# Half-partition loads, one collecting product a unit, and two result stores in a windowed decode attention kernel

## The chip, the cores and the metric

The kernel runs on one core of a Trainium2 chip. The metric is device time in microseconds (us) of one execution. The kernel before takes 218.12 us (median of three runs, 217.67 to 219.65).

A core has five engines that run their own instruction streams and wait for each other through semaphores: PE (TensorE, matrix products; PEld is its loading of weights), DVE (VectorE), ACT (ScalarE), POOL (GpSimd) and SP (SyncE, which here only issues loads and stores). Sixteen DMA engines carry the loads and stores. SBUF, the working memory, has 128 partitions; PSUM takes the products.

## The reference, cut to what matters

Everything is float32. One token for each of two batches (B = 2) goes through a layer norm, then through an attention with 32 query heads on 8 key-value heads over the last 4096 positions of a cache, and through a gated MLP whose result is the gate.

```python
W = min(4096, max(256, Sk // 4))                     # 4096 of 32768 positions
q = (x @ wq).reshape(B, Sq, Hq, Dh).transpose(0, 2, 1, 3)
k = jnp.repeat(k_cache[:, :, Sk - W:, :], rep, axis=1)
v = jnp.repeat(v_cache[:, :, Sk - W:, :], rep, axis=1)
p = _softmax(jnp.einsum("bhqd,bhkd->bhqk", q, k) * (Dh ** -0.5), axis=-1)
o = jnp.einsum("bhqk,bhkd->bhqd", p, v)
s = o.transpose(0, 2, 1, 3).reshape(B, Sq, Hq * Dh) @ wo

z = _gelu(xn @ w_in); z2 = _layernorm(z[..., Fh:])
g = _silu((z[..., :Fh] * (w_sp * z2 + b_sp)) @ w_out)
return x + s * g
```

The inputs that count by size: `w_in` 512 x 1792, `w_out` 896 x 512, `wq` 512 x 4096, `wo` 4096 x 512, and the used 4096 positions of both caches, 8 heads x 2 batches x 4096 x 128 each.

## The kernel before, in words

**Units and loads.** A unit is one key-value head with both batches. Its keys and its values are one load each of 128 partitions x 32 KB (4 MB). SP issues all large loads in one fixed order (lines 94 to 140 and 477 to 485): `win` (3.5 MB), `wout` (1.75 MB), `wq` in two loads of 4 MB, then keys and values of the eight units, the values behind the keys, and at the end `wo`: one load of 4 MB for the first set of units and six smaller ones (1 MB three times, 512 KB, 256 KB twice) for the other two sets. `win`, the two `wq`, all keys and values and the two `wo` tiles share a ring of four slots of 32 KB a partition (`slot`, line 83): a load whose slot is not yet free makes SP wait, and with it every load behind it. Loads also share eight completion semaphores in turn, so a load can wait until the one eight before it has landed.

**Head.** PE computes `z` from `win`, the four slices of the query product from `wq` (`queries`, line 238), and the gate from `wout`.

**One unit.** DVE turns the keys in four pieces (`turn`, 128 x 2048 each), PE makes the scores (16 products), DVE takes the masked row maximum (`row_max`), PE and DVE share it over the groups of rows that hold the same head (`share_max`, `bias`), ACT takes the exponential with the row sums `p.l` (`probs`, line 367), PE reorders the probabilities (`swapped`, which also sums `p.l` over the groups into column NB of `p.mo`), DVE transposes them and makes the weights `p.w = diag / sum` (`probs_t`, lines 382 to 385). Then PE multiplies by the values (`values`, 16 products into `acc`), ACT copies `acc` to `o` with the scale `p.w` (`evacuate`, line 399), and PE collects `o` (`collect`, line 409).

**Collecting.** Units form three sets: units 0 to 3, 4 and 5, 6 and 7 (`SETS`, line 329). For each unit `collect` makes four products, one for each group of 32 rows, into the tile `col`, which adds up over a set; at a set's end DVE reduces `col` to `both` and multiplies by a batch mask to `o1`. `spread` then places the columns for the product with `wo` into `oT`.

**Order.** Every instruction stands in program order on its engine (`InOrder`, line 27). The loop at line 460 interleaves: while unit n is loaded and scored, unit n-1 gets its probabilities and, behind it, its values.

**End.** After the last unit's values (line 505), `evacuate` runs on ACT and DVE in turn, then come the last `collect` and `spread`, then the products with `wo`: `wo_early` for the first 24 tiles of 128 x 512 into `part`, a copy, and four products by `rowm` into `so`; the last eight tiles go straight into `so`. Two DVE instructions (`res`) and one store of eight rows, which lie 16 partitions apart, end the kernel.

## Time and profile before

| what | value |
|---|---|
| median of the runs | 218.12 us |
| the profiled execution's own time | 218.11 us |
| its span, first to last instruction | 216.2 us |
| PE busy | 136.8 us (63%) |
| DVE busy | 103.9 us (48%) |
| ACT busy | 23.9 us (11%) |
| mean busy share of the DMA engines | 97%, 89.4 MB read |
| mean granted TensorE clock | 0.783 |

The page gives busy times of each engine, then the span in 40 equal slices as tenths, then the DMA queues, then the chain of work that ended last. Another view groups the instructions by form, with the mean time of one and what ended the idle time before them; another gives busy time, DMA share and GB/s for chosen stretches. The execution's own time is 1.9 us over its span.

### The profile page before, as it was taken

The numbers are of one execution on the slowest core, as the hardware profiler recorded it, in microseconds if no ns is written. First come the engines' busy times: TensorE is split into PE (matmuls) and PEld (weight loads), VectorE is DVE, ScalarE is ACT, GpSimd is POOL, SyncE is SP. The second block draws the span as 40 slices with busy tenths as digits, with TensorE's granted clock in tenths as the row PEclk, the third lists the DMA queues.
The fourth block names the chain that finished last, engine by engine and source line by source line (L and its number), as shares of the span: only waits on it lengthen the run. The fifth ranks groups of instructions, "written<-read, shape, count | busy, mean of one in ns | idle before, by whom it ended". The sixth has DMA issues, their size and how long they took to land.

```text
span 216.2 us, 2192 instructions
## 1 busy us (share of the span) xinstructions
PE 136.8 (63%) x908; PEld 46.8 (22%) x908; DVE 103.9 (48%) x161; ACT 23.9 (11%) x60; POOL 3.2 (1%) x16
## 2 busy tenths in 40 slices
PE   0172294627765964984593298359667749969683
PEld 0120021113112222222131122122221122342331
DVE  2504014439539638728908921990487197220201
ACT  5003003200001011021021002101010012030010
POOL 5000000000000000000000000000000000000000
PEclk9998569985587595596599559956955787997998
DMA  7999999999999999999999999999999999999990
GB/s 255 425 437 467 406 455 418 423 443 412 455 400 461 409 455 412 436 430 424 449 403 455 412 449 415 430 436 418 455 408 449 418 443 415 443 430 402 409 376 27
DMA packets 3929, 89.54 MB, mean 414 GB/s; under 512 B 446, under 2 KB 462, under 8 KB 848
## 3 DMA queue, kind: packets, MB, share of 16 engines
q1 hardware_dynamic: 3900, 89.40, 96.8%
q8 instruction: 7, 0.11, 0.2%
q10 hardware_dynamic: 20, 0.01, 0.0%
q14 instruction: 2, 0.02, 0.0%
HBM read 89.40 MB, written 0.00 MB: 413 GB/s over the span
## 4 chain that ended last, share of the span: by engine, by line
DMA 62%; DVE 17%; PE 17%; SPq 2%; issue 1%; ACT 0%; DVEq 0%; ACTq 0%
DMA v<-in_A_v_cache_dram 29%; DMA k<-in_A_k_cache_dram 20%; DVE kt L37 13%; DMA wo<-in_A_wo_dram 12%; PE acc L37 9%; PE s L37 7%; SPq L37 2%; PE pp L37 1%; DVE sm L37 1%; DVE pT L37 1%; DVE qw L37 1%; ACT p L37 0%; DVE mg L37 0%; DVE res L37 0%; PE so L37 0%
## 5 line engine op out<-in xcount | busy, mean ns | idle before, releaser
L37 DVE STREAM_TRANSPOSE kt<-k 128x2048 f32<-128x2048 f32 x32 | 72.7, 2293 | 3.4 <-DMA k<-in_A_k_cache_dram 3.4
L37 PE MATMUL acc<-v,pT 128*32 128x512 f32 x256 | 45.3, 863 | 10.9 <-DMA v<-in_A_v_cache_dram 9.6
L37 PE MATMUL s<-kt,qw 128*32 128x512 f32 x256 | 41.1, 684 | 3.7 <-DVE kt L37 3.1
L37 PE MATMUL pp<-p,swap 128*128 128x512 f32 x16 | 12.6, 880 | 21.0 <-ACT p L37 21.0
L37 DVE CUSTOM_DVE_ANT_1 sm<-s,own 128x512 f32<-128x512 f32 x8 | 5.5, 690 | 36.9 <-PE s L37 36.9
L37 PEld LDWEIGHTS acc<-v,pT 128*32 128x32 f32 x256 | 11.5, 159 | 37.4 <-issue 33.4
L37 ACT ACTIVATE o<-acc,wd 128x128 f32<-128x128 f32 x30 | 8.7, 368 | 73.9 <-PE acc L37 67.1
L37 PE MATMUL q_ps<-wq,xnT 128*32 128x512 f32 x64 | 9.6, 723 | 11.2 <-DMA wq<-in_A_wq_dram 11.2
L37 PEld LDWEIGHTS s<-kt,qw 128*32 128x32 f32 x256 | 9.4, 122 | 33.0 <-issue 21.9
L37 ACT ACTIVATE p<-sm,nb 128x512 f32<-128x512 f32 x8 | 5.8, 723 | 69.1 <-DVE nb L37 69.1
L37 DVE STREAM_TRANSPOSE pT<-pp 128x512 f32<-128x512 f32 x8 | 5.7, 706 | 5.8 <-PE pp L37 5.8
L37 PE MATMUL z<-win,xnT 128*32 128x448 f32 x32 | 5.6, 868 | 4.4 <-DMA win<-in_B_w_in_dram 4.4
L37 PE MATMUL mo<-mg,same 128*128 128x16 f32 x16 | 3.2, 273 | 7.7 <-DVE mg L37 7.7
L37 PEld LDWEIGHTS pp<-p,swap 128*128 128x128 f32 x16 | 3.0, 234 | 21.8 <-ACT p L37 21.8
L37 DVE TENSOR_REDUCE both<-col 128x32 f32<-128x128 f32 x3 | 0.9, 292 | 13.4 <-PE col L37 13.4
L37 PEld LDWEIGHTS mo<-l,same 128*128 128x128 f32 x16 | 4.4, 276 | 6.0 <-issue 6.0
L37 ACT ACT_TABLE_LOAD x4 | 5.1, 1283 | 2.6 <-POOL place L206 2.6
L37 PE MATMUL part<-wo,oT 128*32 128x512 f32 x48 | 5.4, 594 | 0.0
L37 PEld LDWEIGHTS q_ps<-wq,xnT 128*32 128x32 f32 x64 | 1.9, 125 | 14.7 <-DMA wq<-in_A_wq_dram 11.4
L37 PE MATMUL xnT_ps<-ident,xn 2*128 2x2 f32 x4 | 0.6, 253 | 7.0 <-DVE xn L37 7.0
L37 PE MATMUL qj_ps<-qT,selj 128*128 128x64 f32 x8 | 2.0, 428 | 4.8 <-DVE qT L37 4.8
L37 DVE STREAM_TRANSPOSE zt<-z 128x448 f32<-128x448 f32 x1 | 1.0, 975 | 8.3 <-ACT z L37 8.3
(106 smaller groups left out, 66.9 us busy)
## 6 DMA issues: line engine op xcount, KB each, us to landing
k<-in_A_k_cache_dram SPq DMA_DIRECT2D x8, 4096.0 KB, 26.4
v<-in_A_v_cache_dram SPq DMA_DIRECT2D x8, 4096.0 KB, 29.7
wq<-in_A_wq_dram SPq DMA_DIRECT2D x2, 4096.0 KB, 24.2
wo<-in_A_wo_dram SPq DMA_DIRECT2D x1, 4096.0 KB
win<-in_B_w_in_dram SPq DMA_DIRECT2D x1, 3584.0 KB, 11.1
wo<-in_A_wo_dram SPq DMA_DIRECT2D x3, 1024.0 KB, 21.7
wout<-in_B_w_out_dram SPq DMA_DIRECT2D x1, 1792.0 KB, 14.9
wo<-in_A_wo_dram SPq DMA_DIRECT2D x1, 512.0 KB
```

The source lines that it names most:

```text
L37: return self.tc.keep_in_program_order(call(*args, **kwargs))
```

## The change

Five things are edited.

1. `wout`, both `wq` loads and the first `wo` tile are loaded by `halves`: one load into partitions 0 to 63 and one into partitions 64 to 127, one behind the other on SP. `win`, the keys, the values and the second `wo` tile are loaded as before.
2. The first `wo` tile is also cut in two pieces of eight 128 x 512 tiles, so it comes in four loads of 1 MB. Its first piece's products (`wo_early(0)`) stand ahead of the last `collect`.
3. For units 0 to 5 `collect` makes one product of 128 x 512 with 128 weight columns in place of four of 128 columns with 32 weight columns; at the end of sets 0 and 1 DVE takes the diagonal blocks out by four reductions of 32 partitions. Units 6 and 7 collect as before.
4. The row sums are no longer divided out unit by unit. `probs` puts them in a column of the set's tile `lt`; at the set's end one product sums them over the groups, and DVE multiplies by `diag`, reduces, takes the reciprocal and applies it with the batch mask in one instruction. `evacuate` scales by the constant `diag`, so the product by `p.l`, the reciprocal `w` and the tile `wd` of each unit go.
5. The result's eight rows stand on two runs of four partitions (30 to 33 and 94 to 97) in place of eight partitions 16 apart; `x4` is loaded and the result is stored in two pieces, the stores by ACT and SP. The tiles `hT`, `oT` and `rowp` have padding columns for this.

```diff
+    def halves(dst, src):
+        for r in (slice(0, P // 2), slice(P // 2, P)):
+            sp.dma_start(dst[r], src[r])
...
-    sp.dma_start(wout, w_out.rearrange("(p j) d -> p j d", p=P))
+    halves(wout, w_out.rearrange("(p j) d -> p j d", p=P))
...
-        sp.dma_start(t, wq_v[:, a : a + 2, :])
+        halves(t, wq_v[:, a : a + 2, :])
...
+    for _, g in PAIRS:
+        act.dma_start(pair(x4, g), of_pair(x, g))
...
     def swapped(p):
         p.pp = bank(f"pp{p.n}", 512)
         pe.matmul(p.pp, swap.rearrange("p g e c -> p (g e c)"), p.p, start=True, stop=True)
-        pe.matmul(p.mo[:, NB : NB + 1], same.rearrange("p n e -> p (n e)"), p.l, start=True, stop=True)
 
     def probs_t(p):
         p.pT = sb.tile([P, CT, 32], F32, tag="pT", name=f"pT{p.n}", bufs=3)
         dve.transpose(p.pT.rearrange("p t m -> p (t m)"), p.pp)
-        w = sb.tile([P, 1], F32, tag="w", name=f"w{p.n}")
-        dve.reciprocal(w, p.mo[:, NB : NB + 1])
-        p.w = sb.tile([P, CH], F32, tag="wd", name=f"wd{p.n}", bufs=3)
-        dve.tensor_scalar_mul(p.w, diag, w)
...
-                act.activation(p.o[:, a, :], p.acc[:, a, :], AF.Copy, scale=p.w[:, a : a + 1])
+                act.activation(p.o[:, a, :], p.acc[:, a, :], AF.Copy, scale=diag[:, a : a + 1])
...
+        if whole:
             pe.matmul(
-                col[0][32 * g : 32 * g + 32], selw[:, SL - E * a0 : SL - E * a0 + 32], p.o[:, :, 32 * g : 32 * g + 32],
-                start=(a0 == 0), stop=(a0 == n - 1),
+                c.rearrange("p a d -> p (a d)"), selw[:, SL - E * a0 : SL - E * a0 + P],
+                p.o.rearrange("p a d -> p (a d)"), start=(a0 == 0), stop=(a0 == n - 1),
             )
...
         if a0 == n - 1:
+            pl = ps.tile([P, 512], F32, tag="mo", name=f"pl{p.n}")[:, :CH]
+            pe.matmul(pl, same.rearrange("p n e -> p (n e)"), lt, start=True, stop=True)
+            lsum = sb.tile([P, CH], F32, tag="lsum", name=f"lsum{p.n}")
+            dve.tensor_mul(lsum, pl, diag)
+            rl = sb.tile([P, 1], F32, tag="rl", name=f"rl{p.n}")
+            dve.reduce_sum(rl, lsum, axis=AX.X)
+            dve.reciprocal(rl, rl)
...
-            for j, n in (((0, 16),), ((0, 4), (4, 4)), ((0, 4), (4, 2), (6, 1), (7, 1)))[i]:
-                sp.dma_start(t[:, a : a + n, :], wo_s[i][:, j : j + n, :])
+            for j, n in (((0, 8), (8, 8)), ((0, 4), (4, 4)), ((0, 4), (4, 2), (6, 1), (7, 1)))[i]:
+                (sp.dma_start if i else halves)(t[:, a : a + n, :], wo_s[i][:, j : j + n, :])
...
     evacuate(units[-1], split=True)
+    wo_early(0)
     gathered(units[-1])
     spread_after(units[-1])
-    for n in range(3):
+    for n in range(1, 4):
         wo_early(n)
...
-    sp.dma_start(bass.AP(tensor=out.tensor, offset=out.offset, ap=by_group), res[0 : P : P // (G * B), :])
+    for engine, g in PAIRS:
+        engine.dma_start(of_pair(out, g), pair(res, g))
```

The loads as SP issues them, from the last values on, before (the shape is partitions x elements; `v_113` is the last unit's values, `wo_836` the first set's tile, `wo_838` the tile of the other two sets):

```order
L37 DMA v_113<-in_A_v_cache_dram 128x1x8192
L37 DMA wo_836<-in_A_wo_dram 128x8192
L37 DMA wo_838<-in_A_wo_dram 128x2048 x3
L37 DMA wo_838<-in_A_wo_dram 128x1024
L37 DMA wo_838<-in_A_wo_dram 128x512 x2
L37 DMA out_dram<-res 4x2x128
```

The first `wo` tile is one load of 128 partitions there. In the changed kernel the same stretch of SP's program reads (`v_117` is the last unit's values, `wo_801` the first set's tile, `wo_806` the other):

```order
L37 DMA v_117<-in_A_v_cache_dram 128x1x8192
L37 DMA wo_801<-in_A_wo_dram 64x4096 x4
L37 DMA wo_806<-in_A_wo_dram 128x2048 x3
L37 DMA wo_806<-in_A_wo_dram 128x1024
L37 DMA wo_806<-in_A_wo_dram 128x512 x2
L37 DMA out_dram<-res 2x2x128
```

The one load has become four of 64 partitions, and half of the result's store has left SP for ACT. The head of SP's program changes in the same way; in the changed kernel, from its first load to the first values (`v_91`), it is:

```order
L37 DMA win<-in_B_w_in_dram 128x7168
L37 DMA wout<-in_B_w_out_dram 64x3584 x2
L37 DMA wq_74<-in_A_wq_dram 64x8192 x2
L37 DMA wq_77<-in_A_wq_dram 64x8192 x2
L37 DMA k_87<-in_A_k_cache_dram 128x1x8192
L37 DMA k_89<-in_A_k_cache_dram 128x1x8192
L37 DMA v_91<-in_A_v_cache_dram 128x1x8192
```

Before, the second to fourth of these rows are single loads of 128 partitions; the order of the tiles is the same. On PE the end of the program before is, from the last unit's values (`acc_907`) to the last product (`col` collects, `oT_ps` spreads, `part` and `so` are the products with `wo`):

```order
L37 MATMUL acc_907<-v_113,pT_890 32x512 x16
L37 MATMUL col_902<-o_924,selw 32x128 x4
L37 MATMUL oT_ps_936<-o_2_329,place_258 128x16 x4
L37 MATMUL part<-wo_836,oT_324 32x512 x16
L37 MATMUL part<-wo_838,oT_327 32x512 x8
L37 MATMUL so<-parts,rowm 32x128 x4
L37 MATMUL so<-wo_838,oT_330 32x128 x32
```

And in the changed kernel, from the last unit's values (`acc_876`):

```order
L37 MATMUL acc_876<-v_117,pT_863 32x512 x16
L37 MATMUL part<-wo_801,oT_332 32x512 x8
L37 MATMUL col_871<-o_893,selw 32x4x32 x4
L37 MATMUL pl_910<-lt_340,same 128x4
L37 MATMUL oT_ps_920<-o_2_339,place_264 128x16 x4
L37 MATMUL part<-wo_801,oT_332 32x512 x8
L37 MATMUL part<-wo_806,oT_337 32x512 x8
L37 MATMUL so<-parts,rowp 32x128 x4
L37 MATMUL so<-wo_806,oT_342 32x128 x32
```

Eight of the sixteen products with the first `wo` tile now stand between the last values and the last collecting products, and the product `pl` stands behind these.

More of the change, by code (lines that the diff above doesn't have):

```diff
@@ L106, with turn_of @@
     act.dma_start(wb1[:, 1:2], bass.AP(tensor=b_sp.tensor, offset=b_sp.offset, ap=[[1, 1], [1, 1]]))
+    PAD = 32 - B
+    PAIRS = ((act, 0), (sp, 2))
+    pair = lambda t, g: t[32 * g + PAD : 32 * g + PAD + 2 * B, :]
+    of_pair = lambda t, g: bass.AP(tensor=t.tensor, offset=t.offset + g * DC, ap=[[DC, 2], [D, B], [1, DC]])
     x4 = cst.tile([P, DC], F32, tag="x4", name="x4")
     nc.gpsimd.memset(x4, 0.0)
-    by_group = [[DC, G], [D, B], [1, DC]]
-    act.dma_start(x4[0 : P : P // (G * B), :], bass.AP(tensor=x.tensor, offset=x.offset, ap=by_group))
+    for _, g in PAIRS:
+        act.dma_start(pair(x4, g), of_pair(x, g))
+    def turn_of(t, j, g):
+        return t[:, 32 * j + PAD * (g % 2) : 32 * j + PAD * (g % 2) + 32]
     def load(name, src, u):
@@ L144 @@
     make_identity(nc, ident)
-    SL = (CH - 1) * E
-    selw = cst.tile([P, SL + 32 + SL - 0], F32, tag="selw", name="selw")
+    SL = 32
+    selw = cst.tile([P, SL + P], F32, tag="selw", name="selw")
     nc.gpsimd.memset(selw, 0.0)
@@ L151 @@
     nc.gpsimd.memset(ones, 1.0)
-    hT = cst.tile([P, FT, 32], F32, tag="hT", name="hT")
+    hT = cst.tile([P, PAD + 32 * FT], F32, tag="hT", name="hT")
     nc.gpsimd.memset(hT, 0.0)
-    rowm = cst.tile([P, 32], F32, tag="rowm", name="rowm")
+    rowp = cst.tile([P, PAD + 32], F32, tag="rowp", name="rowp")
+    nc.gpsimd.memset(rowp, 0.0)
+    rowm = rowp[:, PAD:]
     dve.tensor_reduce(rowm, ident.rearrange("p (g c) -> p c g", g=G), axis=AX.X, op=ALU.add)
@@ L187 @@
     dve.tensor_copy(same, free_ap(selw, SL, [[0, NB], [1, E]]))
+    dve.tensor_copy(free_ap(selw, 2 * SL, [[32, G - 1], [1, E]]), free_ap(selw, SL, [[0, G - 1], [1, E]]))
     blk = cst.tile([P, G], F32, tag="blk", name="blk")
@@ L279 @@
     dve.tensor_scalar(z2, z2, wb[:, 0:1], wb[:, 1:2], op0=ALU.mult, op1=ALU.add)
-    dve.tensor_mul(hT[:, :, 0 : 16 * B : 16], z1, z2)
+    dve.tensor_mul(hT[:, PAD:].rearrange("p (j c) -> p j c", c=32)[:, :, :B], z1, z2)
     queries(2)
@@ L286 @@
         g = j % G
-        pe.matmul(py[32 * g : 32 * g + 32, :], hT[:, j, :], wout[:, j, :], start=(j < G), stop=(j + G >= FT))
+        pe.matmul(py[32 * g : 32 * g + 32, :], turn_of(hT, j, 1), wout[:, j, :], start=(j < G), stop=(j + G >= FT))
     ys = sb.tile([P, D], F32, tag="o", name="ys", bufs=1)
@@ L291 @@
     for g in range(G):
-        pe.matmul(y[32 * g : 32 * g + 32, :], rowm, ys[:, g * DC : (g + 1) * DC], start=True, stop=True)
+        pe.matmul(y[32 * g : 32 * g + 32, :], turn_of(rowp, 0, g), ys[:, g * DC : (g + 1) * DC], start=True, stop=True)
     gate = cst.tile([P, DC], F32, tag="gate", name="gate")
@@ L332 @@
         o1 = cst.tile([P, B, 32], F32, tag=f"o1_{i}", name=f"o1_{i}")
-        oT = cst.tile([P, nj, 32], F32, tag=f"oT_{i}", name=f"oT_{i}")
+        lt = cst.tile([P, CH], F32, tag=f"lt_{i}", name=f"lt_{i}")
+        nc.gpsimd.memset(lt, 1.0)
+        oT = cst.tile([P, PAD + 32 * nj], F32, tag=f"oT_{i}", name=f"oT_{i}")
         nc.gpsimd.memset(oT, 0.0)
         for a in range(n):
-            sets[kv + a] = (a, n, o1)
+            sets[kv + a] = (a, n, o1, lt)
         sets[f"oT{i}"] = (o1, oT, nj)
@@ L368, in probs @@
         p.p = sb.tile([P, CT * 32], F32, tag="p", name=f"p{p.n}", bufs=1)
-        p.l = sb.tile([P, 1], F32, tag="l", name=f"l{p.n}")
+        a0, _, _, lt = sets[p.n]
         act.activation(
-            p.p, p.sm.rearrange("p t y -> p (t y)"), AF.Exp, bias=p.nb, scale=SCALE, accum_out=p.l,
+            p.p, p.sm.rearrange("p t y -> p (t y)"), AF.Exp, bias=p.nb, scale=SCALE, accum_out=lt[:, a0 : a0 + 1],
         )
@@ L402, in evacuate @@
             if split and a % 2:
-                dve.tensor_scalar_mul(p.o[:, a, :], p.acc[:, a, :], p.w[:, a : a + 1])
+                dve.tensor_scalar_mul(p.o[:, a, :], p.acc[:, a, :], diag[:, a : a + 1])
             else:
-                act.activation(p.o[:, a, :], p.acc[:, a, :], AF.Copy, scale=p.w[:, a : a + 1])
+                act.activation(p.o[:, a, :], p.acc[:, a, :], AF.Copy, scale=diag[:, a : a + 1])
     col = {}
     def collect(p):
-        a0, n, o1 = sets[p.n]
+        a0, n, o1, lt = sets[p.n]
@@ L411, in collect @@
+        whole = p.n < SETS[-1][0]
         if a0 == 0:
-            col[0] = ps.tile([P, CH, 32], F32, tag="col", name=f"col{p.n}")
-        for g in range(G):
+            col[0] = ps.tile([P, CH, DH], F32, tag="col", name=f"col{p.n}")
+        c = col[0]
+        if whole:
             pe.matmul(
-                col[0][32 * g : 32 * g + 32], selw[:, SL - E * a0 : SL - E * a0 + 32], p.o[:, :, 32 * g : 32 * g + 32],
-                start=(a0 == 0), stop=(a0 == n - 1),
-            )
-        if a0 == n - 1:
-            both = sb.tile([P, 32], F32, tag="both", name=f"both{p.n}", bufs=1)
-            dve.reduce_sum(both, col[0].rearrange("p a j -> p j a"), axis=AX.X)
-            dve.tensor_mul(o1, free_ap(both, 0, [[0, B], [1, 32]]), free_ap(ofb, 0, [[1, B], [0, 32]]))
+                c.rearrange("p a d -> p (a d)"), selw[:, SL - E * a0 : SL - E * a0 + P],
+                p.o.rearrange("p a d -> p (a d)"), start=(a0 == 0), stop=(a0 == n - 1),
+            )
+        else:
+            for g in range(G):
+                pe.matmul(
+                    c[32 * g : 32 * g + 32, :, :32], selw[:, SL - E * a0 : SL - E * a0 + 32],
+                    p.o[:, :, 32 * g : 32 * g + 32], start=(a0 == 0), stop=(a0 == n - 1),
+                )
@@ new lines, in collect @@
+        if a0 == n - 1:
+            pl = ps.tile([P, 512], F32, tag="mo", name=f"pl{p.n}")[:, :CH]
[5 more added lines that the diff above has]
+            dve.reciprocal(rl, rl)
+            both = sb.tile([P, 32], F32, tag="both", name=f"both{p.n}", bufs=1)
+            if whole:
+                for g in range(G):
+                    rows, cols = slice(32 * g, 32 * g + 32), slice(32 * g, 32 * g + 32)
+                    dve.reduce_sum(both[rows], c[rows, :, cols].rearrange("p a j -> p j a"), axis=AX.X)
+            else:
+                dve.reduce_sum(both, c[:, :, :32].rearrange("p a j -> p j a"), axis=AX.X)
+            dve.scalar_tensor_tensor(
+                out=o1, in0=free_ap(both, 0, [[0, B], [1, 32]]), scalar=rl, in1=free_ap(ofb, 0, [[1, B], [0, 32]]),
+                op0=ALU.mult, op1=ALU.mult,
+            )
@@ L432, in spread @@
             )
-        dve.tensor_copy(oT[:, :, 0 : 16 * B : 16], pt.rearrange("p b j -> p j b"))
+        dve.tensor_copy(oT[:, PAD:].rearrange("p (j c) -> p j c", c=32)[:, :, :B], pt.rearrange("p b j -> p j b"))
     ends = {kv + n - 1: i for i, (kv, n, nj) in enumerate(SETS)}
@@ L494, in wo_early @@
             pe.matmul(
-                part[32 * g : 32 * g + 32, :], oT[:, j + a, :], t[:, a, :], start=(done < G), stop=(done >= EARLY - G)
+                part[32 * g : 32 * g + 32, :], turn_of(oT, j + a, 1), t[:, a, :], start=(done < G), stop=(done >= EARLY - G)
             )
@@ L514 @@
     for g in range(G):
-        pe.matmul(so[32 * g : 32 * g + 32, :], rowm, parts[:, g * DC : (g + 1) * DC], start=True, stop=False)
-    for n in range(3, len(blocks)):
+        pe.matmul(so[32 * g : 32 * g + 32, :], turn_of(rowp, 0, g), parts[:, g * DC : (g + 1) * DC], start=True, stop=False)
+    for n in range(4, len(blocks)):
         t, oT, j = blocks[n]
@@ L520 @@
                 pe.matmul(
-                    so[32 * g : 32 * g + 32, :], oT[:, j + a, :], t[:, a, g * DC : (g + 1) * DC],
-                    start=False, stop=(j + a == oT.shape[1] - 1),
+                    so[32 * g : 32 * g + 32, :], turn_of(oT, j + a, g), t[:, a, g * DC : (g + 1) * DC],
+                    start=False, stop=(n == len(blocks) - 1 and a == t.shape[1] - 1),
                 )
```

## The prediction

> **What bounds the kernel now.** I read the page first: its slices of DMA and GB/s, then the chain that ended last, then the DMA issues; after that the stretches of the span, and last the instructions at the end. The page:

> ```profile
> span 216.2 us, 2192 instructions
> PE 136.8 (63%) x908; PEld 46.8 (22%) x908; DVE 103.9 (48%) x161; ACT 23.9 (11%) x60; POOL 3.2 (1%) x16
> DMA  7999999999999999999999999999999999999990
> GB/s 255 425 437 467 406 455 418 423 443 412 455 400 461 409 455 412 436 430 424 449 403 455 412 449 415 430 436 418 455 408 449 418 443 415 443 430 402 409 376 27
> DMA 62%; DVE 17%; PE 17%; SPq 2%; issue 1%; ACT 0%; DVEq 0%; ACTq 0%
> ```

> No compute engine is near full. The DMA engines are over 90% busy in 38 of 40 slices, and only the first and the last slice are below. So the time is a ramp, a stream without a gap, and what follows the last landing. The stretches (microseconds from the span's start, then busy time of PE, PEld, DVE, ACT and POOL, granted clock, DMA share, GB/s) give the stream's rate:

> ```profile
> 16.10:25.80 9.70, 1.72 (x14) 0.52 (x6) 2.62 (x10) 2.05 (x3) 0.00 (x0) 0.71 1.00 432
> 11.80:35.50 23.70, 12.39 (x70) 3.69 (x70) 4.42 (x21) 3.74 (x6) 0.00 (x0) 0.78 1.01 436
> 35.50:192.70 157.20, 107.09 (x648) 35.55 (x649) 91.78 (x110) 15.89 (x47) 0.00 (x0) 0.75 1.00 430
> 192.70:202.40 9.70, 7.34 (x59) 2.90 (x58) 2.41 (x8) 0.73 (x2) 0.00 (x0) 0.82 0.97 413
> 202.40:212.50 10.10, 8.93 (x120) 3.95 (x120) 0.18 (x1) 0.60 (x1) 0.00 (x0) 1.00 0.84 340
> 212.50:216.20 3.70, 0.42 (x8) 0.16 (x8) 0.58 (x2) 0.00 (x0) 0.00 (x0) 0.80 0.00 1
> ```

> From 11.8 to 192.7 us the share is 1.00 and the rate 430 to 436 GB/s, whatever is loaded: 27 GB/s for each of 16 engines that are all busy. Any microsecond that the engines lose in the stream is a microsecond of the kernel.

> How far the compute side may fall behind without being seen is in the DMA issues (KB each, median us from issue to landing):

> ```profile
> k<-in_A_k_cache_dram SPq DMA_DIRECT2D x8, 4096.0 KB, 26.4
> v<-in_A_v_cache_dram SPq DMA_DIRECT2D x8, 4096.0 KB, 29.7
> wq<-in_A_wq_dram SPq DMA_DIRECT2D x2, 4096.0 KB, 24.2
> win<-in_B_w_in_dram SPq DMA_DIRECT2D x1, 3584.0 KB, 11.1
> wout<-in_B_w_out_dram SPq DMA_DIRECT2D x1, 1792.0 KB, 14.9
> ```

> 4 MB take 9.7 us at 432 GB/s, but land 26.4 us after their issue: 16.7 us of other loads lie ahead. A slot that comes free some microseconds later starves nothing. The end, in order of time (start, us, engine):

> ```profile
> 185.47 26.99 DMA wo<-in_A_wo_dram
> 212.46 0.04 issue
> 212.50 0.47 PE so L37 x8
> ...
> 213.00 0.30 DVE res L37
> 213.30 0.02 issue
> 213.32 0.29 DVE res L37
> ```

> The last piece of `wo` lands at 212.46; eight matrix instructions, two of DVE and the store follow, 3.7 us to the span's end at 216.2. The profiled execution took 218.11 us by its own time, 1.9 us over its span, and 218.12 is the median of the runs, so sums made on it carry over without a shift.

> **The change, part by part.** *The halves.* Stretch 11.8 to 35.5 is exactly `wout` and both `wq` (`win` lands at 0.7 + 11.1 = 11.8): 10.2 MB in 23.7 us. Stretch 192.7 to 202.4 is the first `wo` tile: 4.2 MB in 9.7 us. All 33.4 us become loads of 64 partitions, one half behind the other. The trace has no wide load into fewer than 128 partitions, so I bound the cost. Lower end: an engine carries 27 GB/s whatever its partitions, a half of 2 MB takes 4.85 us, and nothing is lost: 0 us. Upper end: the ceiling belongs to the ways into the partitions. In every row above each of 16 engines has an eighth of a 128-partition tile to itself; when all 16 are sent to 64 partitions, two share a way, each gets 13.5 GB/s, and 33.4 us become 66.8: +33.4 us. The reading that chooses is the rate: it is 432 for the 32 KB rows of `wq`, which lie side by side in memory, and 430 over keys and values, which alternate between two batches far apart. A limit that doesn't move with the source's layout sits rather at the engine or at the destination, and these two the trace cannot part. I take the upper end, because a half changes just what those rows have in common, all partitions at once.

> [...]

> From the upper end I take off what engines out of step give back. If of two that share a way one is t us ahead, it runs alone for t at the start of a half, and has gone over to the other half while its partner still finishes: each half costs t less. In the stretch of 202.4 to 212.5 the share is 0.84: an engine is idle for 0.16 x 10.1 = 1.6 us on average, which is how far engines lie apart there; in the stretches up to 192.7 shares of 1.00 leave a few tenths. Six halves early at 0.2 us give 1.2, four late ones at some 0.3 us (partners less apart than the whole field, and the slowest pair sets the end) give 1.2. Halves: 33.4 - 2.4 = **+31 us**. There is no cover: nothing else is bound.

> *The extra issues.* SP issues five more loads, and the second half of the first `wq` now waits for `win` to land, since eight loads share eight semaphores; `wo`'s last pieces wait so for its first halves. Rows for an issue:

> ```profile
> 1.18 0.41 SPq L37 DMA_DIRECT2D wout<-in_B_w_out_dram  x1
> 1.63 1.25 SPq L37 DMA_DIRECT2D wq<-in_A_wq_dram  x2
> ```

> 0.4 to 0.6 us each, with the whole of `wout` and half a `wq` still queued at 11.8 us, and 3 MB of `wo` when its first halves land. 0 us; without that cover, one issue, 0.6 us.

> *Collecting and sums.* The rows (mean ns of one):

> ```profile
> L37 PE MATMUL col<-o,selw 128*32 128x128 f32 x64 | 3.8, 285 | 1.7 <-DVE o L37 1.7
> L37 PE MATMUL pp<-p,swap 128*128 128x512 f32 x16 | 12.6, 880 | 21.0 <-ACT p L37 21.0
> L37 PE MATMUL mo<-l,same 128*128 128x1 f32 x16 | 3.0, 258 | 0.0
> L37 DVE RECIPROCAL w<-mo 128x1 f32<-128x1 f32 x8 | 1.0, 130 | 0.0
> L37 DVE TENSOR_SCALAR wd<-diag,w 128x4 f32<-128x4 f32 x8 | 1.8, 230 | 0.3
> L37 DVE TENSOR_REDUCE both<-col 128x32 f32<-128x128 f32 x3 | 0.9, 292 | 13.4 <-PE col L37 13.4
> ```

> A product of 128 x 512 with 128 columns is the form of `pp`: 12.6 / 8 = 1.6 us, for 3.8 / 8 = 0.5 before: six times +1.1 = 6.6 us of PE. Eight products by `p.l` go, -3.0, and three `pl` come, at most +1.1: PE +4.7 us of 136.8. DVE loses 8 x 0.36 = 2.9 us, and gains per set a multiply, a reduce and a reciprocal (0.5 us by rows of that size) and, in two sets, three more reductions of 0.29: 1.5 + 1.7 = 3.2. All this lies in a stream with 16.7 us queued ahead: 0 us. Only the last set could be seen: `pl` and 0.5 us of DVE ahead of the last `spread`, while eight early products (half of 16 x 0.11 x 2) fill PE's idle before the last `collect`. The products then still wait for `wo`: in the row above, the last ones start 0.04 us behind the landing. 0 us; without that wait, some +0.8 - 1.8 = -1 us.

> *Store and rows.* Two stores of 2 KB on two engines replace one of 4 KB, whose row is

> ```profile
> 213.64 0.69 SPq L37 DMA_DIRECT2D out_dram<-res  x1
> ```

> Between -0.3 (half the rows to issue) and +0.7 (one behind the other); I take 0, as they are issued side by side. One more `x4` load costs ACT some 0.6 us ahead of the layer norm, which has the 4.4 us that PE waits for `win`:

> ```profile
> L37 PE MATMUL z<-win,xnT 128*32 128x448 f32 x32 | 5.6, 868 | 4.4 <-DMA win<-in_B_w_in_dram 4.4
> ```

> Sum: 218.1 + 31 = **249 us**.

> **The rivals.** *The engine is the limit, not the way (not slower).* Then halves run at 432 GB/s, and everything else is under the stream: 218.1, with the store's bounds 217.8 to 219. For it: an engine at 27 GB/s is at the same figure in every row, which a limit of its own would give too. Against it: nothing in the trace, only the choice above. It decides as soon as two engines at one way get over 13.5 GB/s each; at 27 all cost is gone. Within it the end may gain: engines lie apart by 1.6 us in the last stretch, and if halves hand the late ones' rows round, up to 1.6 us go: 216.5, still under 1%.

> *The engines fall out of step.* If one of each pair is favoured, or they start 1.6 us apart from the beginning, a half of `wout` (2.1 us) costs 0.5, of `wq` (4.85) 3.25, a quarter of `wo` (2.4) 0.8: 1 + 13 + 3.2 = 17 us, 235 us. Against it: the shares of 1.00 and more in the early stretches.

> *A new wait shows.* The load order is the same, but a semaphore of eight comes round sooner; if SP were late with the first keys, the stream would have a gap of one landing, about 2 to 5 us: 221 to 223. Against it: at each such wait more than 2 MB are queued.

> **How the numbers follow.** Shared ways at nearly half rate: 0.61, 245 to 252. Out of step or in part: 0.06, 225 to 245. Engine-limited, unchanged: 0.29, 217 to 219.5. A new wait: 0.02. Faster by over 1%: 0.02; the stream's bytes and rate leave no room for 2.2 us but by the end alone. The range must hold the second case too: 217 to 252; the likeliest alone has 245 to 252. 1% is about what a measurement of this kernel tells from no change: faster 0.02, same 0.29, slower 0.69.

> **What would show it.** In the changed profile the stretches of `wout`, `wq` and the first `wo` tile have 200 to 230 GB/s with a DMA share still near 1 (engines wait with a packet in hand), the first keys land near 69 us in place of 46.6, keys and values run at 430 again, and the end behind the last landing is 3.7 us. If those stretches show 430, the rival holds and the step that took the upper end is wrong. I am also wrong if keys and values run slower than before, if DMA shares fall below 0.9 between loads (a wait), or if the last products of `so` no longer follow a landing.

## The result, and the profile after

The changed kernel takes 255.4 us (median of six runs, 254.41 to 256.33) against 218.2 us: a ratio of 1.169 (95% interval 1.164 to 1.174), +37 us. The forecast was 249 us with a range up to 252: the direction came, and the main mechanism with it, but the price was set too low. The profiled execution took 256.24 us by its own time, over a span of 254.4.

The page of the changed kernel, with the lines that were shown of before:

```profile
span 254.4 us, 2120 instructions
PE 140.8 (55%) x862; PEld 45.0 (18%) x862; DVE 104.7 (41%) x161; ACT 23.9 (9%) x60; POOL 3.5 (1%) x20
DMA  7999999898999999999999999999999999999990
GB/s 289 368 228 229 206 206 227 185 232 316 443 404 422 443 453 410 417 443 443 428 417 430 453 422 422 433 443 425 428 429 443 425 422 397 198 214 207 274 371 29
DMA 66%; PE 17%; DVE 13%; ACT 1%; issue 1%; SPq 1%; another core or an unknown queue 0%; ACTq 0%; DVEq 0%
...
wq<-in_A_wq_dram SPq DMA_DIRECT2D x4, 2048.0 KB, 28.1
wo<-in_A_wo_dram SPq DMA_DIRECT2D x7, 1024.0 KB, 37.3
```

The DMA line reads as before: 8 or 9 tenths from the second slice to the last but one. The line under it does not. In slices 3 to 9 and 35 to 37 the same busy engines move 185 to 232 GB/s. The trace's records of single packets show how both can be: over `wq` each of the 256 packets of 32 KB took 1.21 us before, and 2.57 us in the median now, and all of that time counts as busy. GB/s shows what the share hides. It isn't that fewer engines carry a half: the share, 1.00 over `wq`, is a mean over all sixteen. The trace also has sixteen completion marks (semaphore updates that report a load's end) for each of these loads, as it has for a whole one; over `wout` and `wq` the first and the last of them lie 1.0 us apart.

The stretches of the same execution, cut at the landings of `win` (12.8), `wout` (21.0), `wq` (60.9), the first keys (70.5), the values of unit 6 (208.0) and of unit 7 (220.5), the first `wo` tile (240.6) and the rest of `wo` (250.4); columns as before:

```profile
12.80:21.00 8.20, 5.11 (x34) 1.70 (x34) 2.13 (x9) 1.02 (x3) 0.00 (x0) 1.00 1.02 221
21.00:60.90 39.90, 7.22 (x36) 2.04 (x36) 3.67 (x21) 2.73 (x4) 0.00 (x0) 0.57 1.00 213
60.90:70.50 9.60, 7.49 (x56) 2.30 (x57) 2.38 (x6) 1.50 (x3) 0.00 (x0) 0.84 0.99 427
70.50:208.00 137.50, 92.53 (x504) 27.00 (x506) 85.75 (x82) 12.54 (x38) 0.00 (x0) 0.76 1.00 432
208.00:220.50 12.50, 8.43 (x65) 3.64 (x56) 3.81 (x14) 1.84 (x6) 0.00 (x0) 0.88 1.01 329
220.50:240.60 20.10, 10.77 (x66) 4.77 (x66) 1.83 (x8) 0.73 (x2) 0.00 (x0) 0.67 0.99 222
240.60:250.40 9.80, 8.28 (x97) 2.84 (x97) 0.00 (x0) 0.60 (x1) 0.00 (x0) 0.78 0.76 306
250.40:254.40 4.00, 0.42 (x8) 0.15 (x8) 0.58 (x2) 0.00 (x0) 0.00 (x0) 1.00 0.00 1
```

Two stretches of before that the prediction doesn't show by themselves, `wout` and the last values:

```profile
11.80:16.10 4.30, 4.14 (x24) 1.35 (x28) 0.00 (x0) 0.00 (x0) 0.00 (x0) 1.00 1.05 452
183.00:192.70 9.70, 8.05 (x73) 3.07 (x66) 1.54 (x6) 2.57 (x9) 0.00 (x0) 1.00 1.01 432
```

Set against before, the span's 38.2 us come out piece by piece. `win` lands 1.0 later. `wout` takes 8.2 in place of 4.3 (+3.9). Both `wq` take 39.9 in place of 19.4 (+20.5). From there to the landing of the last values the stream takes 159.6 in place of 157.2 (+2.4), and all of that is the last piece: 12.5 us for a load of 4 MB that takes 9.7 everywhere else. The first `wo` tile takes 20.1 in place of 9.7 (+10.4); the rest of `wo` 9.8 in place of 10.1 (-0.3); what follows the last landing 4.0 in place of 3.7 (+0.3). The sum is 38.2.

The last values' load is not cut in halves. It is the one ahead of halves, and the shared rate of 329 GB/s shows that it ran into them. Its completion marks say the same: the first comes 9.8 us behind the first of the load before it (205.8 to 215.6), so the leading engine lost nothing, and the last 12.5 us behind the last (208.0 to 220.5). PE waited 2.5 us for it:

```profile
220.65 5.50 PE L37 MATMUL acc<-v,pT 128*32 128x512 f32 x32 [2.53 <-DMA v<-in_A_v_cache_dram]
```

### The profile page after: what moved, and what is told of

The parts are those of the page before. It is cut to its first block, busy times and chain, and to the rows that moved or that the text cites. A ratio compares the mean times of both kernels' runs of the same rounds, so it can differ in the third digit from the quotient of the medians.

```text
span 254.4 us, 2120 instructions
## 1 busy us (share of the span) xinstructions
PE 140.8 (55%) x862; PEld 45.0 (18%) x862; DVE 104.7 (41%) x161; ACT 23.9 (9%) x60; POOL 3.5 (1%) x20
## 4 chain that ended last, share of the span: by engine, by line
DMA 66%; PE 17%; DVE 13%; ACT 1%; issue 1%; SPq 1%; another core or an unknown queue 0%; ACTq 0%; DVEq 0%
DMA v<-in_A_v_cache_dram 25%; DMA wq<-in_A_wq_dram 18%; DMA wo<-in_A_wo_dram 18%; DVE kt L37 9%; PE acc L37 7%; PE s L37 5%; DMA win<-in_B_w_in_dram 5%; PE pp L37 2%; PE q_ps L37 1%; ACT p L37 1%; DVE pT L37 1%; DVE sm L37 1%; DVE gate L37 1%; PE ys L37 1%; SPq L37 1%
## 5 line engine op out<-in xcount | busy, mean ns | idle before, releaser
L37 DVE STREAM_TRANSPOSE kt<-k 128x2048 f32<-128x2048 f32 x32 | 72.5, 2286 | 0.3 <-DMA k<-in_A_k_cache_dram 0.3
L37 PE MATMUL acc<-v,pT 128*32 128x512 f32 x256 | 43.8, 845 | 16.1 <-DMA v<-in_A_v_cache_dram 12.3
L37 PE MATMUL s<-kt,qw 128*32 128x512 f32 x256 | 38.9, 654 | 4.4 <-DVE kt L37 2.9
L37 PE MATMUL q_ps<-wq,xnT 128*32 128x512 f32 x64 | 11.7, 871 | 35.7 <-DMA wq<-in_A_wq_dram 35.7
L37 PE MATMUL pp<-p,swap 128*128 128x512 f32 x16 | 11.4, 798 | 21.2 <-ACT p L37 21.2
L37 DVE CUSTOM_DVE_ANT_1 sm<-s,own 128x512 f32<-128x512 f32 x8 | 5.5, 692 | 37.5 <-PE s L37 37.4
L37 PEld LDWEIGHTS acc<-v,pT 128*32 128x32 f32 x256 | 11.2, 158 | 47.2 <-issue 40.7
L37 ACT ACTIVATE o<-acc,diag 128x128 f32<-128x128 f32 x30 | 8.7, 367 | 77.0 <-PE acc L37 76.6
L37 PEld LDWEIGHTS s<-kt,qw 128*32 128x32 f32 x256 | 9.3, 118 | 32.1 <-issue 20.7
L37 PE MATMUL part<-wo,oT 128*32 128x512 f32 x48 | 8.1, 827 | 8.2 <-DMA wo<-in_A_wo_dram 8.2
L37 ACT ACTIVATE p<-sm,nb 128x512 f32<-128x512 f32 x8 | 5.8, 723 | 65.6 <-DVE nb L37 65.6
L37 DVE TENSOR_REDUCE mean<-mean_ps 128x2 f32<-128x14 f32 x1 | 0.2, 173 | 23.7 <-PE mean_ps L37 23.7
L37 PEld LDWEIGHTS q_ps<-wq,xnT 128*32 128x32 f32 x64 | 2.5, 145 | 40.2 <-issue 40.2
L37 DVE TENSOR_TENSOR lsum<-pl,diag 128x4 f32<-128x4 f32 x3 | 0.5, 162 | 19.6 <-PE pl L37 19.6
L37 PE MATMUL col<-o,selw 128*32 128x128 f32 (+1 forms) x28 | 8.1, 510 | 0.0
L37 DVE STREAM_TRANSPOSE pT<-pp 128x512 f32<-128x512 f32 x8 | 5.7, 714 | 4.6 <-PE pp L37 4.4
L37 PE MATMUL z<-win,xnT 128*32 128x448 f32 x32 | 4.8, 763 | 4.6 <-DMA win<-in_B_w_in_dram 4.6
L37 PEld LDWEIGHTS pp<-p,swap 128*128 128x128 f32 x16 | 2.8, 219 | 22.0 <-ACT p L37 22.0
L37 PE MATMUL mo<-mg,same 128*128 128x16 f32 x16 | 3.2, 273 | 5.8 <-DVE mg L37 5.4
L37 DVE TENSOR_SCALAR gate<-y 128x128 f32<-128x128 f32 x1 | 0.3, 291 | 14.6 <-PE y L37 14.6
L37 DVE TENSOR_TENSOR res<-so,gate 128x128 f32<-128x128 f32 x1 | 0.3, 291 | 14.2 <-PE so L37 14.2
## 6 DMA issues: line engine op xcount, KB each, us to landing
k<-in_A_k_cache_dram SPq DMA_DIRECT2D x8, 4096.0 KB, 23.5
v<-in_A_v_cache_dram SPq DMA_DIRECT2D x8, 4096.0 KB, 25.2
win<-in_B_w_in_dram SPq DMA_DIRECT2D x1, 3584.0 KB, 12.1
```

The source lines that it names most:

```text
L37: return self.tc.keep_in_program_order(call(*args, **kwargs))
```

## The experiments

**Is it the halves? Taken back, and alone.** The first run keeps the whole change but loads whole tiles:

```diff
     def halves(dst, src):
-        for r in (slice(0, P // 2), slice(P // 2, P)):
-            sp.dma_start(dst[r], src[r])
+        sp.dma_start(dst, src)
```

> The changed kernel with the halves taken back: wout, both wq and the two pieces of the first wo tile are single loads of 128 partitions; everything else of the change stays. Theory A (a load into 64 partitions runs at half rate, and this is the whole loss): 218 us, 217.5 to 219, wq at 430 GB/s, first keys landing at 46.6 us. Theory B (collecting, sums, early products or the two stores cost part of the 37 us): 221 us or more, with the excess behind 192 us of the trace.

Measured: 218.65 us, ratio 1.0016 (1.0004 to 1.0029). Its stretches of `wout`, of `wq` and about the first `wo` tile:

```profile
12.20:16.50 4.30, 4.16 (x24) 1.35 (x28) 0.00 (x0) 0.00 (x0) 0.00 (x0) 1.00 1.02 437
16.50:35.90 19.40, 9.31 (x50) 2.44 (x42) 3.98 (x18) 3.74 (x6) 0.00 (x0) 0.72 1.01 437
192.60:202.40 9.80, 8.64 (x74) 3.31 (x66) 1.66 (x7) 0.73 (x2) 0.00 (x0) 0.84 1.00 420
```

The second run puts the halves alone on the kernel before, by the same two lines at `wout`, `wq` and the first `wo` tile, which stays one piece.

> The kernel before with one edit: wout, both wq and the first wo tile (one piece) in two loads of 64 partitions each. Theory A: 255 us (254 to 256.5), as the whole change; first keys at 70 us, wq near 210 GB/s. Theory B: less than 250.

Measured: 257.02 us, ratio 1.1774 (1.1759 to 1.1789), so a little more than the whole change. From `wout`'s landing to that of `wq`, and then over the last values and over the `wo` tile:

```profile
21.30:61.40 40.10, 6.92 (x36) 1.92 (x36) 3.35 (x20) 2.36 (x4) 0.00 (x0) 0.56 1.00 210
208.70:221.30 12.60, 9.12 (x73) 4.66 (x64) 2.72 (x10) 1.84 (x6) 0.00 (x0) 0.84 1.07 337
221.30:241.00 19.70, 6.43 (x48) 2.53 (x48) 1.40 (x5) 0.73 (x2) 0.00 (x0) 0.67 0.94 195
```

So the halves are the loss. Beside whole loads, collecting, sums, early products and the two stores together cost 0.4 us (0.1 to 0.6 by the interval). Theory B falls. Halves alone came out 0.5 us above the 254 to 256.5 that was expected, and 1.6 us above the whole change; whether the rest of the change gains that beside halves is open.

**Partitions, or just more and smaller loads?** The changed kernel with as many loads of the same sizes, but cut across the row (`wout`, with its odd first dimension, by its 512 columns, so that its runs in memory are 1 KB):

```diff
-        for r in (slice(0, P // 2), slice(P // 2, P)):
-            sp.dma_start(dst[r], src[r])
+        n = dst.shape[1] // 2
+        if dst.shape[1] % 2:
+            sp.dma_start(dst[:, :, : dst.shape[2] // 2], src[:, :, : dst.shape[2] // 2])
+            sp.dma_start(dst[:, :, dst.shape[2] // 2 :], src[:, :, dst.shape[2] // 2 :])
+        else:
+            sp.dma_start(dst[:, :n], src[:, :n])
+            sp.dma_start(dst[:, n:], src[:, n:])
```

> The changed kernel with each of these tiles still in two loads, as many and as large as in the change, but of 128 partitions and half of the row. Theory A (partitions): 218 us, 217.5 to 219.5. Theory C (more, smaller loads and the earlier reuse of semaphores are what costs): 250 us or more, since count, size and waits of the loads are those of the change.

Measured: 219.83 us, ratio 1.0094 (1.0068 to 1.0119). Its slices:

```profile
GB/s 249 422 352 422 434 431 440 456 404 464 404 458 410 443 416 440 428 428 440 422 443 410 458 398 470 398 458 401 458 405 464 404 452 413 440 384 420 419 384 27
```

One slice, the third, in which `wout` comes in 1 KB runs, has 352 GB/s; `wq` beside it is at full rate. Count, size and semaphore waits of the loads are those of the change, and the 36 us are not there. Theory C falls. The time is 0.3 us above Theory A's range; 1.2 us over the whole loads are left, and most of them lie in the third slice, which is some 0.9 us short of its neighbours' bytes.

**How many partitions, or which?** The changed kernel with each of these tiles in three loads, partitions 32 to 95, then 0 to 31, then 96 to 127:

```diff
-        for r in (slice(0, P // 2), slice(P // 2, P)):
+        for r in (slice(32, 96), slice(0, 32), slice(96, P)):
```

> The changed kernel with each of these loads cut into partitions 32 to 95, then 0 to 31, then 96 to 127. [...] Theory A2 (how many partitions: 64 give half the rate, 32 a quarter): 9.7 + 9.7 + 9.7 a tile, +67 us: 285 us.

Measured: 243.26 us, ratio 1.1159. That is 42 us under the 285 of A2. Over the first 25.7 of the 32.3 us of `wq`

```profile
20.30:46.00 25.70, 7.06 (x36) 2.00 (x36) 2.70 (x15) 3.20 (x5) 0.00 (x0) 0.59 1.03 266
```

the rate is 266 GB/s, and over the whole of `wq` 260, 16.1 us for a tile of 4.2 MB. With the middle piece at full rate and the quarters at half it would be some 14.7 us (an estimate from the 432 GB/s of before and the 213 of the change). The completion marks tell the pieces apart. The quarters took 4.4 to 5.4 us each, where 1 MB at 213 GB/s is 4.9. The middle piece took 5.6 us from first mark to first mark and 6.7 to 6.8 from last to last, where full rate is 4.9 and a half of 64 partitions in the change takes 10.0. So position plays a part, and the three pieces run into each other. This also speaks against a limit at the source: the middle piece reads 64 neighbouring rows of `wq`, as the change's halves do, and only its partitions lie elsewhere. A cleaner cut settled the rest: every second partition, on the kernel before, for `wout` and both `wq`, with this line in `halves`:

```diff
-        for r in (slice(0, P // 2), slice(P // 2, P)):
+        for r in (slice(0, P, 2), slice(1, P, 2)):
```

> The kernel before with early halves cut the other way: partitions 0, 2, ... 126, then 1, 3, ... 127, again 64 each. [...] If 64 partitions are slow by their number: 243.

Measured: 218.46 us, ratio 1.0011 (1.0000 to 1.0022): nothing lost. Its stretches of `wout` and `wq`:

```profile
12.00:16.30 4.30, 4.30 (x28) 1.38 (x32) 0.00 (x0) 0.00 (x0) 0.00 (x0) 1.00 1.04 445
16.30:35.50 19.20, 7.44 (x50) 2.08 (x42) 4.66 (x22) 3.74 (x6) 0.00 (x0) 0.73 1.01 437
```

Loads of 64 partitions, of the same bytes, rows, count and semaphores as the change's, run at 437 GB/s when their partitions are spread over the whole SBUF, and at 213 when they lie in one half of it. So neither the number of partitions nor the engine is the limit; what the runs have left is where the partitions of a load lie. Why that counts, no trace here shows. The case that 64 partitions are slow by their number (243 us) fell.

**Do the parts add up?** Halves for the early loads alone, and for the first `wo` tile alone, on the kernel before:

> The kernel before with halves for wout and both wq alone. If the parts add up: 218.3 + 25.3 = 243.6 us (243 to 245), 25.3 being what the changed kernel's trace lost up to the landing of wq; the end as before. If early and late losses interact: outside 242 to 246.

> The kernel before with halves for the first wo tile alone (one piece, two loads of 2 MB). By the prediction's step (engines out of step give something back): 218.3 + 9.7 - 1.2 = 227 us or less. If being out of step costs instead, as the changed kernel's trace has it (the last values land 2.8 us later, halves behind them 10.3 us more): 218.3 + 13 = 231 us (230 to 232.5).

Measured: 243.33 us (ratio 1.1139, 1.1095 to 1.1184) and 230.77 us (1.0566, 1.0518 to 1.0615). So +25.2 and +12.6, together 37.8, against 38.8 for halves alone and 37.2 for the change. The late ones lie within the 230 to 232.5 us of the case that being out of step costs, not at the 227 or less at which it gives back. From the landing of unit 6's values in the late run:

```profile
183.00:195.50 12.50, 8.83 (x75) 5.18 (x67) 2.72 (x10) 1.84 (x6) 0.00 (x0) 0.85 1.05 336
195.50:215.30 19.80, 6.59 (x48) 2.53 (x48) 1.40 (x5) 0.73 (x2) 0.00 (x0) 0.67 0.95 198
```

12.5 us for the last values and 19.8 behind them; the changed kernel has 12.5 and 20.1.

**Does the side matter?** The late halves alone, with the upper half first:

```diff
-        for r in (slice(0, P // 2), slice(P // 2, P)):
+        for r in (slice(P // 2, P), slice(0, P // 2)):
```

> As the run with late halves alone, but partitions 64 to 127 first. Theory: engines that are ahead start on the first half while late engines still write the last values, and share the late ones' ways; which of them suffer depends on the side. If the late engines of the last values sit on both sides: 231 us as before. If they sit on the lower side alone: the last values land near 10 us after the ones before them in place of 12.5, and the time is 228 to 229. If the order plays no part and late engines simply cost: 231.

Measured: 233.09 us, ratio 1.0675 (1.0616 to 1.0734), with 13.5 us for the last values:

```profile
183.40:196.90 13.50, 9.71 (x87) 4.27 (x79) 2.72 (x10) 2.20 (x8) 0.00 (x0) 0.90 1.04 316
```

That is not the 228 to 229 of late engines on the lower side alone, and not the 231 of the other two cases either: the loss stays on either side, and is 2 us larger here. Why it is larger is open.

**Do engines out of step give back or cost?** An extra load of eight rows behind `win` (the trace has eight completion marks for it) puts engines behind, once with early halves and once with whole loads:

```diff
+    wq0 = slot("wq0", 2, HQ * DH)
+    sp.dma_start(wq0[0 : P : 16], wq.rearrange("(p k) f -> p k f", p=P)[0 : P : 16, 0:2, :])
     wout = cst.tile([P, FT, D], F32, tag="wout", name="wout")
...
+        t = wq0 if a == 0 else slot(f"wq{a}", 2, HQ * DH)
```

> The kernel before with early halves and, behind win, one extra load of eight rows of wq (partitions 0, 16, ... 112; loaded again by the wq loads): eight of the sixteen engines get one more row of 32 KB each and are some 2 us behind the others when the halves begin. To be set against the next run, which has the extra load with whole loads. If being out of step gives time back at each half, as the prediction had it: 20 us or less over the next run. If it neither gives nor costs: 25.2 over it. If it costs at the change from whole loads to halves, as at the last values: 27 or more over it.

> The kernel before with the extra load of eight rows alone. The eight late engines carry their delay of some 1.2 to 2.4 us through the stream to the end: 219.3 to 220.8 us. If they catch up: 218.3.

Measured: 248.0 us and 221.26 us, 26.7 apart, against 25.2 without the extra load. The 20 us or less that giving back would need is excluded; 26.7 lies between "neither" and "27 or more", and with intervals of some 0.6 to 1 us on each of these times a cost of 1.5 us is not firm. The whole-load run came out 0.5 us above its range. The completion marks put the step itself to the test: the engines end half a `wq` 0.8 us apart in the run with early halves alone, 1.0 in the changed kernel and 4.2 here, and each of the first three halves takes 10.0 us in all three runs.

**Would two queues use both sides at once?** The lower half from SP, the upper from ACT, early loads only; these loads also stand behind the small loads of ACT in the program now:

```diff
-        for r in (slice(0, P // 2), slice(P // 2, P)):
-            sp.dma_start(dst[r], src[r])
+        sp.dma_start(dst[: P // 2], src[: P // 2])
+        act.dma_start(dst[P // 2 :], src[P // 2 :])
```

> The kernel before with early halves, the lower half issued by SP and the upper by ACT, so each of the sixteen engines has both halves waiting in two queues (the small loads on ACT go first). If engines take from the two queues in turn and so keep all ways busy: 218 to 222 us, and win lands later, since ACT's halves run beside it. If they march through the same half together whatever the queue: 243 us.

Measured: 243.77 us, ratio 1.1167 (1.1108 to 1.1225), the same as from one queue. With halves waiting in both queues the rate from 20 to 60 us is 241 GB/s:

```profile
20.00:60.00 40.00, 13.25 (x74) 4.13 (x74) 8.27 (x41) 6.71 (x10) 0.00 (x0) 0.74 1.01 241
```

(this stretch also holds other loads).

**The change, mended.** The whole changed kernel with every second partition in place of the two contiguous halves, at `wo` as well:

> The whole changed kernel with one difference: its halves are every second partition (0, 2, ... 126, then 1, 3, ... 127), at wout, both wq and both pieces of the first wo tile. If contiguous halves were the whole loss, also at the end of the stream where the engines lie 2 us apart: 218.7 us (218.3 to 219.3), as the changed kernel with whole loads. If going from whole loads to halves costs in itself when engines lie apart: 220.5 or more, with the last values landing over 11 us after the ones before them.

Measured: 218.58 us, ratio 0.9997 (0.9975 to 1.0019). At the place that cost 12.5 and 20.1 us, the last values and the first `wo` tile:

```profile
183.00:192.70 9.70, 7.92 (x58) 3.65 (x56) 3.81 (x14) 1.84 (x6) 0.00 (x0) 1.00 0.97 416
192.70:202.50 9.80, 8.61 (x65) 3.58 (x66) 1.66 (x7) 0.74 (x2) 0.00 (x0) 0.83 0.99 418
```

The completion marks of a load lie 2.2 us apart there, as in the changed kernel ahead of its halves. So going over to 64-partition loads where engines lie 2 us apart costs nothing in itself; the cost came only where a half lies on one side (12.5 us for the last values, 9.7 here). No run here is faster than the kernel before by more than its interval: the stream's bytes at its rate are the time, as the first reading had it.

## Why the prediction was right and wrong

**Right: what bounds the kernel.** The microseconds lost in the stream add up to the time, and the middle of the stream ran unchanged (432 GB/s from 70.5 to 208.0).

**Right: halves at half rate, by choice of the upper end.** `wq` ran at 213 GB/s, inside the 200 to 230 that was to show it, with a DMA share of 1.00; the first keys landed at 70.5 us (69 foretold). The rival that the engine is the limit falls with this: the same sixteen engines, busy all the time, carried half. The run with every second partition shows that 64 partitions alone don't do it: there each engine had its 27 GB/s. The argument I chose by, that the rate doesn't depend on the source's layout, left engine and destination open, and the trace of before could not part them. (The pieces of `wq` also lie 64 KB apart in memory, not side by side as that argument has it.) That two engines share a way, on which the upper end rests, no run shows; the runs show 213 GB/s for a half on one side and 437 for every second partition.

**Wrong: "from the upper end I take off what engines out of step give back".** That step set -2.4 us and so +31. Nothing was given back: half a `wq` takes 10.0 us whether its engines lie 0.8 or 4.2 us apart, where the step has t less for engines t apart. In its place stands a cost. Where whole loads pass into halves, the whole load ahead landed late: +2.8 us at the last values, and +1.0 at `win`, of which up to 0.6 may be something else, since `win` landed at 12.0 to 12.4 in the three runs of the changed kernel with whole loads, column halves and every second partition. That the leading engines were already writing the first half while the others still had the whole load to finish fits the completion marks of the last values. Halves alone, late halves, the other side first and the added delay all show a cost or none, never a gain. Why engines out of step gain nothing is open: which engine takes which rows of a 64-partition load isn't seen in the trace. The measure was wrong too: I read how far engines lie apart from the DMA share, with a few tenths where it is 1.00. By the completion marks of before they lie 0.6 us apart up to `wq`, and 1.9 to 2.1 us over all keys and values, at a share of 1.00.

**Wrong: 33.4 us as an upper end.** I doubled the time and took it for a bound. The halves themselves cost 3.9 + 20.5 + 10.4 = 34.8 us, 1.4 over it, since `wq` and `wo` ran a little under half rate (19.4 to 39.9, and 9.7 to 20.1; a packet of `wq` took 2.57 us in the median where twice 1.21 is 2.43). Why they ran under it is open. With the 3.8 us at the changes that is 38.6; -0.3 in the rest of `wo`, +0.3 behind it and -0.4 in the stream's middle make the 38.2. The range's top of 252 stood on that end and missed 255.4.

**Right: the parts at nothing.** The change with whole loads is at 1.0016, and mended at 0.9997. PE is busy 4.0 us longer than before, where I had 4.7, and DVE 0.8, where I had 0.3. From the groups of the changed kernel:

```profile
L37 PE MATMUL col<-o,selw 128*128 128x512 f32 x12 | 6.8, 645 | 0.0
L37 PE MATMUL pl<-lt,same 128*128 128x4 f32 x6 | 1.2, 262 | 0.0
L37 DVE TENSOR_REDUCE both<-col 32x32 f32<-32x128 f32 x8 | 2.3, 282 | 0.1
```

The six wide products took 6.8 us in all, 1.1 each where I had 1.6 by `pp`; the small reductions 282 ns each, as 0.29. All lay under the stream. The store: 4.0 us behind the last landing in place of 3.7, inside -0.3 to +0.7. The wait for earlier loads' semaphores is in the trace (the loads name eight, and the second half of the first `wq` is issued at 12.85 us, when `win`'s last mark stands at 12.83). It opened no gap: the DMA share is 0.99 to 1.02 from `win`'s landing to the end of the first `wo` tile, and the run with column halves has the same waits at full rate. Two slips in the text change no sum: SP issues six more loads, not five, and a sixteenth of the tile, not an eighth, is what each of sixteen engines has (in the 9.7 us of a tile an engine has time for eight packets of 1.21 us, and the tile has 128).

**The rival "out of step"** (235 us), by which half a `wq` takes 8.1 us, fell with the step it came from; "a new wait" did not show.

## What to carry to other kernels

## What the hardware showed that I had not expected

Loads of 64 partitions lost nothing when the partitions were every second one (437 GB/s, 218.46 us), although such a load carries the same bytes as a contiguous half, which ran at 213. And the place where whole loads pass into halves has a price of its own, for the load that is not cut: 12.5 us in place of 9.7 for the last values, 13.5 with the upper half first, 9.7 again with every second partition.
